# Attention and two MoE layers on one core: decoding of the weights in fewer and denser steps, a third split buffer, output copies after both halves of a PSUM tile

## The chip, the core and the metric

The kernel runs on one core of a Trainium2 chip. Five engines work beside each other, each in the order of its own instructions: TensorE (PE in the profile; PEld is its weight load), VectorE (DVE), ScalarE (ACT), GpSimd (POOL) and SyncE (SP), which here issues every DMA. The metric is the device time of one execution in microseconds.

## The reference

```python
# attention: q, k, v are 4 x 8 x 576 x 64
scores = scale * np.matmul(q, k.transpose(0, 1, 3, 2)) + bias   # bias: a small network of relative positions
attn = np.exp(scores - np.max(scores, axis=-1, keepdims=True))
attn = attn / (np.sum(attn, axis=-1, keepdims=True) + 1e-09)
x = np.matmul(attn, v)                      # as 2304 tokens x 512
h = np.maximum(np.maximum(x @ w1, x @ w2), x @ w3)    # moe1: 512 -> 768
x = h @ w_out                               # 768 -> 512
h = x @ w_in                                # moe2: 512 -> 2048
g = np.where(h > 0.0, h, np.exp(np.minimum(h, 0.0)) - 1.0)
out = g @ w_out2                            # 2048 -> 512
```

The weights of both MoE layers come as float64 and reach the chip as pairs of 32-bit words.

## The kernel before

**Stages.** First the position bias is made, then attention runs in 80 steps (16 pairs of heads, five chunks of rows), then moe1, then moe2. Python code writes the instructions out in order; no scheduler changes it, so the order of the calls is the order on each engine.

**Precision.** Every matrix product is made of three: each operand is split into a high part and a low part, and high x high, high x low and low x high are added in PSUM.

**Decoding.** A block of weights (128 x 512 doubles) is fetched into one of two buffers `raw` (`fetch`, L346). Five VectorE instructions and one of ScalarE turn it into floats (L392 to L402): x_t from the high words, on ScalarE the exponent step L394, t_w or cw_t in four steps, of which the last needs ScalarE's x_t. `split` then writes the high part with ScalarE (L74) and the low part with GpSimd (L80), and `store` sends both to a scratch tensor `scw_...` (L437). `load_w` brings them back into one of six buffers `w_t` (L464) some four products ahead of their use. Splits go to a ring of two buffers `sp2` (sp in the profile). Two kinds don't: a block of w1 that is the very next one needed is split straight into a `w_t` buffer, and w_out of moe1 stays in the tile wo_t. For w_in of moe2 the two halves of a block (keys `("wi", f, 1)` and `("wi", f, 0)`, tile cw_t) get four sums first (L412), and then four splits follow one another: moe2 multiplies by a scheme with sums of sub-matrices.

`decoder` is a generator: each `yield` ends a step, and `pump(k)` advances it by k steps. There are 24 blocks of moe1 (18 of w1, six of w_out) and eight groups of four for moe2. Before, a block costs six steps and a group 32, 400 in all. Attention calls `pump()` in 59 of its steps, on the first twelve blocks alone; `moe1_ev` pumps two steps ahead of each of its evictions, `moe1_out` five behind each. If a load needs a block that isn't decoded, `need` advances the decoder on the spot.

**moe1.** Three passes over 768 tokens. A pass has 18 products (`moe1_mm`, L491: six row blocks, three matrices; 24 instructions each), each into one pair of four pairs of PSUM banks; `moe1_ev` copies the first to a_t on ScalarE (L501), takes the maximum with the other two on VectorE (L503), and splits it into hh and hl. The output stage `moe1_out` (L586, four products of 36 instructions) of one pass runs three products into the next pass, and the last one at the end of moe1; its evictions are xh on ScalarE (L592) and xl on VectorE (L593).

**moe2.** 24 units (three passes, eight blocks of hidden rows). The products L662 go to the two banks Y and X, and VectorE copies them out as c_t, p_t, q_t, u_t. In the first two units each bank is used alternately, and `sums` holds 16 closures that make the four sums of x (e_t on GpSimd, d_t and tt on VectorE and ScalarE): one is called after each of the four turns of the first unit, three after each of the second. The output products L706 add up over the eight units in six banks `acc`: acc[0] and acc[1] are the halves of one two-bank tile (pb), acc[2] and acc[3] of another, acc[4] and acc[5] are tiles of their own. In the last unit of a pass `store_out` copies each to o_t, even ones with VectorE and odd ones with ScalarE, and stores it. The tiles of moe2 take over the memory in which the decoder's buffers lay.

## Time and profile before

| | |
|---|---|
| median of 3 runs | 1043.83 us (1040.75 to 1044.81) |
| the profiled execution | 1043.28 us |
| its span, first to last instruction | 1041.5 us |
| mean granted TensorE clock | 0.989 of 2.4 GHz |
| TensorE busy | 97% of the span |
| DMA, mean over the span | 190 GB/s |

The span leaves out 1.8 us of the execution around the instructions. The clock is that which TensorE was granted, as a share of its full speed; it has two levels, 1.2 and 2.4 GHz. Attention lasts to about 340 us, moe1 to 643 us, moe2 to the end.

### The profile page before, as it was taken

The page shows a single profiled execution, that of the slowest core. Times are in us where ns is not written, and L with a number is a line of the kernel's source. Part 1 is how long each engine was busy: PE and PEld are TensorE (multiplying, and loading weights), DVE is VectorE, ACT ScalarE, POOL GpSimd, SP SyncE. Part 2 cuts the span into 40 slices and gives each one's busy share as a digit, 9 for nine tenths or more (in the row PEclk, how much of TensorE's full clock was granted, in tenths as well). Part 3 has the DMA queues.
Part 4 walks back from the last instruction along what each step waited for, and adds up shares of the span by engine and source line. Part 5 has one row for each costly group of instructions (what it writes and reads, how often), then busy time and mean ns, then how long its engine had stood idle before and what let it go on. Part 6 is the DMA issues. An engine that isn't in the chain of part 4 may idle for free. (4 is left out here: it accounts for less than half of the span.)

```text
span 1041.5 us, 17213 instructions
## 1 busy us (share of the span) xinstructions
PE 1008.3 (97%) x6068; PEld 839.6 (81%) x6068; DVE 691.0 (66%) x1402; ACT 547.1 (53%) x1175; POOL 346.7 (33%) x319
## 2 busy tenths in 40 slices
PE   7999999999999999989998988999999999999997
PEld 3456666666668999989998988879998989889896
DVE  7967778777776699577677755854774356843342
ACT  8978888888885333333232433444444345443443
POOL 0013333333332344335332532522452233522221
PEclk9989999999999999999999999899999999999999
DMA  7741625436232567589767884346557555566552
GB/s 274 270 143 62 224 87 184 143 116 211 96 98 92 171 222 250 166 280 306 275 210 240 293 301 155 111 145 199 175 190 259 183 183 188 192 238 191 170 195 102
DMA packets 67733, 197.65 MB, mean 190 GB/s; under 512 B 9280, under 2 KB 16320, under 8 KB 67648
## 3 DMA queue, kind: packets, MB, share of 16 engines
q1 hardware_dynamic: 67648, 196.56, 56.2%
q8 instruction: 49, 0.80, 0.3%
q14 instruction: 36, 0.29, 0.1%
HBM read 148.16 MB, written 48.37 MB: 189 GB/s over the span
## 5 line engine op out<-in xcount | busy, mean ns | idle before, releaser
L80 POOL TENSOR_TENSOR gl<-t_t,gh 128x384 fp32r<-128x384 f32 x96 | 106.2, 1116 | 246.1 <-ACT gh L74 239.8
L233 DVE CUSTOM_DVE_ANT_0 e_t<-pb,b_t 128x576 f32<-128x576 f32 x144 | 104.1, 756 | 57.1 <-PE pb L224 35.8
L250 POOL TENSOR_SCALAR e_t<-e_t,st_t 128x576 f32<-128x576 f32 x64 | 65.9, 1030 | 225.8 <-DVE st_t L244 213.3
L74 ACT ACTIVATE p<-bk 128x512 f32<-128x512 f32 (+2 forms) x224 | 98.9, 472 | 54.8 <-PE bk L257 54.5
L706 PE MATMUL pb<-w_t,gh 128*128 128x512 f32 x384 | 120.0, 394 | 4.3 <-DVE o_t L76 4.3
L491 PE MATMUL pb<-xh,w_t 128*128 128x384 f32 x448 | 118.4, 340 | 2.7 <-DMA w_t<-scw_w 2.7
L238 ACT ACTIVATE e_t<-e_t,st_t 128x576 f32<-128x576 f32 x144 | 111.7, 776 | 2.2 <-DVE st_t L233 2.2
L491 PE MATMUL bk<-xh,w_t 128*128 128x384 f32 x416 | 109.0, 337 | 3.6 <-DMA w_t<-scw_w 3.0
L684 ACT ACTIVATE t_t<-c_t 128x384 f32<-128x384 f32 x96 | 50.0, 521 | 111.3 <-DVE c_t L675 88.8
L662 PE MATMUL bk<-tt,w_t 128*128 128x384 f32 x528 | 107.5, 338 | 1.0 <-DVE p_t L76 1.0
L662 PE MATMUL bk<-xh,w_t 128*128 128x384 f32 x328 | 96.6, 341 | 6.9 <-DVE c_t L76 6.9
L662 PEld LDWEIGHTS bk<-tt,w_t 128*128 128x128 f32 x528 | 95.0, 188 | 8.8 <-DVE p_t L76 1.4
L491 PEld LDWEIGHTS pb<-xh,w_t 128*128 128x128 f32 x448 | 82.2, 190 | 3.4 <-ACT a_t L501 3.0
L224 PE MATMUL pb<-kq_t 64*128 64x288 f32 x512 | 82.9, 437 | 1.3 <-DVE st_t L233 1.3
L706 PEld LDWEIGHTS pb<-w_t,gh 128*128 128x128 f32 x384 | 70.2, 188 | 13.0 <-DVE o_t L76 6.6
L491 PEld LDWEIGHTS bk<-xh,w_t 128*128 128x128 f32 x416 | 75.4, 188 | 4.0 <-issue 3.3
L491 PE MATMUL pb<-xl,w_t 128*128 128x384 f32 x224 | 76.0, 339 | 0.0
L299 PE MATMUL bk<-p,tv_t 128*64 128x320 f32 (+1 forms) x512 | 76.0, 418 | 0.0
L706 PE MATMUL pb<-w_t,gl 128*128 128x512 f32 x192 | 75.5, 393 | 0.0
L74 ACT ACTIVATE gh<-t_t 128x384 fp32r<-128x384 f32 x96 | 48.9, 519 | 47.2 <-DVE t_t L692 47.2
L692 DVE SCALAR_TENSOR_TENSOR t_t<-t_t,c_t 128x384 f32<-128x384 f32 x96 | 72.1, 769 | 0.8 <-ACT t_t L685 0.5
L662 PEld LDWEIGHTS bk<-xh,w_t 128*128 128x128 f32 x328 | 61.5, 191 | 10.6 <-DVE c_t L76 7.7
(116 smaller groups left out, 2109.4 us busy)
## 6 DMA issues: line engine op xcount, KB each, us to landing
w_t<-scw_w SPq DMA_DIRECT2D x90, 512.0 KB, 4.2
w_t<-scw_wi SPq DMA_DIRECT2D x74, 512.0 KB, 4.2
scw_wi<-sp SPq DMA_DIRECT2D x26, 512.0 KB, 2.9
scw_w<-sp SPq DMA_DIRECT2D x22, 512.0 KB, 5.2
raw<-wo SPq DMA_DIRECT2D x22, 512.0 KB, 4.3
scr<-o_t SPq DMA_DIRECT2D x36, 288.0 KB, 3.9
kq_t<-tkq SPq DMA_DIRECT2D x16, 640.0 KB, 4.8
raw<-wm SPq DMA_DIRECT2D x18, 512.0 KB, 3.7
```

The costliest lines, as they stand in the source:

```text
L74: nc.scalar.activation(dst, src, AF.Copy)
L80: e.tensor_tensor(out=dst, in0=src, in1=hi.bitcast(F32), op=ALU.subtract)
L224: mm(PB[h][:, o], t[r, 640 + 128 * c:768 + 128 * c], t[r, k0:k0 + 288], start=True, stop=True)
L233: nc.vector.tensor_tensor_reduce(out=E[s][:, 576 * h:576 * h + 576], in0=PB[h][:, 224:800], in1=BT[n // 4, c, h], op0=ALU.add, op1=ALU.min ...
L238: nc.scalar.activation(e, e, AF.Exp, bias=st[:, h:h + 1], scale=-1.0, accum_out=st[:, 2 + h:3 + h])
L250: nc.gpsimd.tensor_scalar(e, e, r, 1.0, op0=ALU.mult, op1=ALU.mult)
L299: mm(XO[64 * h:64 * h + 64, 0:w], v[:, 128 * k + 64 * h:128 * k + 64 * h + 64], ps[h][:, k, :], start=(k == 0), stop=False, skip_group_che ...
L491: mm(ps[blk][:, 0:NB], wt[:, ks], xt[:, kk, t0:t0 + NB], start=(j == 0), stop=(j == 11))
L662: mm(ps, w[wt][:, ks], b[xt][:, kk], start=(start and j == 0), stop=(stop and j == 5), skip_group_check=True)
L684: nc.scalar.activation(t, c, AF.Relu, scale=-1.0)
L692: pend.append([lambda: nc.vector.scalar_tensor_tensor(out=t, in0=t, scalar=-1.0, in1=c, op0=ALU.add, op1=ALU.max), last])
L706: mm(acc[t], g[:, ts], w[k], start=(f == 0 and i == 0 and j == 0), stop=(f == NU - 1 and i == 1 and j == 2))
```

## The change

A block's last empty step goes away, so that it costs five steps and a group 31 (368 in all), and each of the last three splits of a burst gets one more step ahead of it. The evictions of moe1's products pump three and two steps, those of its output stages four. `fetch` is called a step later, ahead of the last of the five VectorE instructions instead of behind the fourth. After the attention, every third split that isn't written in place goes to a third buffer, sp3. `store_out` gets a tile of its own for each 128 x 512 block (four instead of two of twice the size) and is called for both halves of a two-bank tile behind the product into the second. In moe2's first two units two closures of `sums` are called a turn.

```diff
@@ -349,6 +349,7 @@
 
     lim = [12]
     WPRE2 = []
+    NSP = [0]
     SCW, WO, HERE, WS, WN = {}, [], set(), [], [0, 0]
 
     def split(key, src, c0=0):
@@ -361,7 +362,9 @@
             WN[0] += 1
             HERE.add(key)
         else:
-            sp2 = wpre.tile([128, 2, 512], F32R, tag="sp2", name="sp2", bufs=2)
+            pool, tag = (WPRE2[0], "sp3") if WPRE2 and NSP[0] % 3 == 2 else (wpre, "sp2")
+            sp2 = pool.tile([128, 2, 512], F32R, tag=tag, name=tag, bufs=2 if tag == "sp2" else 1)
+            NSP[0] += bool(WPRE2)
         hi, lo, src = sp2[:, 0, c0:], sp2[:, 1, c0:], src[:, c0:]
         parts = [partial(hi_of, "a", hi, src), partial(lo_of, "p", lo, src, hi)]
         if key[0] != "wo":
@@ -397,8 +400,8 @@
             nc.vector.scalar_tensor_tensor(out=t, in0=hi, scalar=-0x80000000, in1=t, op0=ALU.bitwise_and, op1=ALU.bitwise_or)
             yield
             nc.vector.scalar_tensor_tensor(out=t, in0=lo, scalar=29, in1=t, op0=ALU.logical_shift_right, op1=ALU.bitwise_or)
+            yield
             fetch()
-            yield
             nc.vector.tensor_tensor(out=t, in0=t, in1=x, op=ALU.bitwise_or)
             if key[0] != "wi":
                 split(key, dst)
@@ -412,10 +415,11 @@
                     nc.vector.tensor_tensor(out=d, in0=a, in1=b, op=op)
                 for p in range(4):
                     yield
+                    if p:
+                        yield
                     split(("wi", key[1], p), cw[:, p], 256 if p == 3 and key[1] > 1 else 0)
                     if len(todo) > 1:
                         store()
-            yield
             yield
             if len(todo) > 1:
                 store()
@@ -495,7 +499,7 @@
         ps = PS.pop((th, m, w))
         for blk in range(2):
             p = ps[blk][:, 0:NB]
-            pump(2)
+            pump(3 - blk)
             if w == 0:
                 A1[blk] = wpre.tile([128, NB], F32, tag="a", name="a_t", bufs=3)
                 nc.scalar.activation(A1[blk], p, AF.Copy)
@@ -591,7 +595,7 @@
                     xh, xl = XH[:, m, t0:t0 + NB], XL[:, m, t0:t0 + NB]
                     nc.scalar.activation(xh, p, AF.Copy)
                     nc.vector.tensor_tensor(out=xl, in0=p, in1=xh.bitcast(F32), op=ALU.subtract)
-                    pump(5)
+                    pump(4)
 
         with tc.manual_schedule():
             order = [(th, m, w) for th in range(3) for m in range(NM1) for w in range(3)]
@@ -705,24 +709,24 @@
         for j, (g, k) in enumerate(((GH, 0), (GH, 1), (GL, 0))):
             mm(acc[t], g[:, ts], w[k], start=(f == 0 and i == 0 and j == 0), stop=(f == NU - 1 and i == 1 and j == 2))
 
-    def store_out(blk, t, o):
+    def store_out(blk, t):
+        o = mp.tile([128, 512], F32, tag="o", name="o_t", bufs=4)
         r0 = blk * TB + 128 * t
         w = 256 if t == 5 else 512
         for c0 in range(0, 512, w):
             cs = slice(c0, c0 + w)
-            hi_of("a" if t % 2 else "v", o[:, t % 2, cs], acc[t][:, cs])
-            nc.sync.dma_start(out[r0:r0 + 128, cs], o[:, t % 2, cs])
+            hi_of("a" if t % 2 else "v", o[:, cs], acc[t][:, cs])
+            nc.sync.dma_start(out[r0:r0 + 128, cs], o[:, cs])
 
     acc = PAIR[0] + PAIR[1] + PAIR[2]
-    OT = {}
 
     def outs(u, i, ts, w):
         for t in ts:
             moe2_out(u, i, t, w, acc)
             if u[1] == NU - 1 and i == 1:
-                if t % 2 == 0:
-                    OT[0] = mp.tile([128, 2, 512], F32, tag="o", name="o_t", bufs=2)
-                store_out(u[0], t, OT[0])
+
+                for d in ((t - 1, t) if t in (1, 3) else (t,) if t > 3 else ()):
+                    store_out(u[0], d)
 
     sums = [fn for i in range(4) for fn in comb(0, i + 1)]
     with tc.manual_schedule():
@@ -748,7 +752,7 @@
                         elu(u, i, q, c)
                         if pre:
                             outs(pre, i, range(3 * q, 3 * q + 3), v)
-                        for _ in range(3 if pre else 1):
+                        for _ in range(2):
                             sums.pop(0)()
                     loads(2 if pre else 1)
                 continue
```

**A burst of splits.** ScalarE in moe1's second pass, at the four splits of the third group (f = 2); sp_... are the split buffers, cw_t the block, a_t and hh evictions. Before:

```order
L74 ACTIVATE sp_5028<-cw_t 128x512
L74 ACTIVATE sp_5033<-cw_t 128x512
L501 ACTIVATE a_t<-bk_866 128x384
L74 ACTIVATE sp_5066<-cw_t 128x512
L74 ACTIVATE sp_5071<-cw_t 128x256
L394 ACTIVATE x_t<-x_t,rebias 128x512
L74 ACTIVATE hh<-a_t 128x384
L74 ACTIVATE sp_5117<-t_w 128x512
```

After:

```order
L74 ACTIVATE sp_4885<-cw_t 128x512
L74 ACTIVATE sp_4917<-cw_t 128x512
L74 ACTIVATE hh<-a_t 128x384
L74 ACTIVATE sp_4925<-cw_t 128x512
L74 ACTIVATE hh<-a_t 128x384
L74 ACTIVATE sp_4961<-cw_t 128x256
L397 ACTIVATE x_t<-x_t,rebias 128x512
L505 ACTIVATE a_t<-pb_100 128x384 x2
L74 ACTIVATE sp_5006<-t_w 128x512
```

The splits of the burst were in two pairs with one eviction between; now evictions stand between the second, third and fourth, and this burst comes two row blocks earlier in the pass.

**The end of moe1.** ScalarE in the last output stage, up to its last eviction; xh are the evictions of that stage. Before:

```order
L74 ACTIVATE sp_6429<-cw_t 128x512
L592 ACTIVATE xh<-bk_866 128x384
L74 ACTIVATE sp_6436<-cw_t 128x512
L74 ACTIVATE sp_6441<-cw_t 128x512
L74 ACTIVATE sp_6446<-cw_t 128x256
L592 ACTIVATE xh<-pb_100 128x384
L394 ACTIVATE x_t<-x_t,rebias 128x512
L74 ACTIVATE sp_6497<-t_w 128x512
L592 ACTIVATE xh<-pb_100 128x384
L394 ACTIVATE x_t<-x_t,rebias 128x512
L74 ACTIVATE sp_6512<-t_w 128x512
L592 ACTIVATE xh<-pb_99 128x384 x2
```

After, from the last product ahead of the stage:

```order
L505 ACTIVATE a_t<-bk_865 128x384
L505 ACTIVATE a_t<-bk_866 128x384
L74 ACTIVATE hh<-a_t 128x384 x2
L596 ACTIVATE xh<-bk_863 128x384
L596 ACTIVATE xh<-bk_864 128x384
L596 ACTIVATE xh<-bk_865 128x384
L596 ACTIVATE xh<-bk_866 128x384
L596 ACTIVATE xh<-pb_100 128x384 x2
L596 ACTIVATE xh<-pb_99 128x384 x2
```

Six splits and two exponent steps stood between these evictions; now there is none.

**The output.** TensorE in the last pass, the first four of the six output products of the last half unit (pb_100 holds acc[0] and acc[1], pb_99 the next two), with what an instruction waits for. Before:

```order
L706 MATMUL pb_100<-w_t,gh 128x512 [waits DMAHW4_49,Activation_49]
L706 MATMUL pb_100<-w_t,gh 128x512
L706 MATMUL pb_100<-w_t,gl 128x512 [waits Pool_49]
L706 MATMUL pb_100<-w_t,gh 128x512 [waits DVE_49]
L706 MATMUL pb_100<-w_t,gh 128x512
L706 MATMUL pb_100<-w_t,gl 128x512
L706 MATMUL pb_99<-w_t,gh 128x512 x2
L706 MATMUL pb_99<-w_t,gl 128x512
L706 MATMUL pb_99<-w_t,gh 128x512 [waits DVE_49]
L706 MATMUL pb_99<-w_t,gh 128x512
L706 MATMUL pb_99<-w_t,gl 128x512
```

After:

```order
L710 MATMUL pb_100<-w_t,gh 128x512 [waits DMAHW2_49,Activation_49]
L710 MATMUL pb_100<-w_t,gh 128x512
L710 MATMUL pb_100<-w_t,gl 128x512 [waits Pool_49]
L710 MATMUL pb_100<-w_t,gh 128x512 x2
L710 MATMUL pb_100<-w_t,gl 128x512
L710 MATMUL pb_99<-w_t,gh 128x512 x2
L710 MATMUL pb_99<-w_t,gl 128x512
L710 MATMUL pb_99<-w_t,gh 128x512 x2
L710 MATMUL pb_99<-w_t,gl 128x512
```

The second product into each two-bank tile waited for VectorE; now it does not.

With the denser steps twelve blocks instead of almost ten are decoded in the attention; the last six blocks of w1, which were split straight into weight buffers, are now ready before their turn and go through the scratch tensor; and the last step of decoding falls three products ahead of the last output stage.

## Rows read from the trace of the kernel before

**Rows 1.** The page: busy us (share) x instructions of each engine.

```profile
PE 1008.3 (97%) x6068; PEld 839.6 (81%) x6068; DVE 691.0 (66%) x1402; ACT 547.1 (53%) x1175; POOL 346.7 (33%) x319
```

**Rows 2.** TensorE's waits, whole span: total us, times, longest us.

```profile
PE bk L662 <- DVE c_t L76: 6.9, 2, 5.6
PE pb L706 <- DVE o_t L76: 4.3, 6, 1.0
PE bk L491 <- DMA w_t<-scw_w: 3.0, 1, 3.0
PE pb L491 <- DMA w_t<-scw_w: 2.7, 1, 2.7
PE bk L586 <- ACT hh L74: 1.9, 1, 1.9
PE bk L586 <- POOL hl L80: 1.5, 1, 1.5
```

**Rows 3.** Windows: us, then each engine's busy us (x instructions), TensorE's clock, DMA share, GB/s.

```profile
460.00:470.00 10.00, 7.80 (x36) 7.83 (x37) 9.79 (x14) 4.36 (x9) 4.90 (x5) 0.83 1.01 370
620.00:630.00 10.00, 10.00 (x50) 10.00 (x50) 7.53 (x14) 3.44 (x6) 0.77 (x2) 0.84 0.59 186
650.00:660.00 10.00, 6.88 (x28) 6.89 (x29) 6.51 (x9) 4.52 (x9) 2.86 (x2) 0.66 0.30 105
```

**Rows 4.** The same view over most of moe1.

```profile
345.00:612.00 267.00, 261.31 (x1497) 260.73 (x1496) 196.85 (x300) 91.81 (x174) 107.27 (x87) 0.99 0.72 243
```

**Rows 5.** ScalarE's waits from 345 to 612 us: total us, times, longest us.

```profile
ACT sp L74 <- DMA scw_wi<-sp: 35.5, 18, 3.8
ACT sp L74 <- DMA scw_w<-sp: 29.1, 6, 6.5
```

**Rows 6.** Timeline of SyncE's DMA queue at 457 us: start, us, instruction.

```profile
457.19 0.46 SPq L464 DMA_DIRECT2D w_t<-scw_w  x1
```

**Rows 7.** Timeline of TensorE and VectorE at moe2's start: start, us, instruction [idle before, releaser].

```profile
643.23 0.33 PE L662 MATMUL bk<-xh,w_t 128*128 128x384 f32 x1
652.50 0.56 DVE L76 COPY c_t<-bk 128x384 f32<-128x384 f32 x1 [2.30 <-DMA scw_w<-sp]
653.12 0.69 PE L662 MATMUL bk<-xh,w_t 128*128 128x384 f32 x1 [5.57 <-DVE c_t L76]
679.82 0.45 PE L662 MATMUL bk<-xh,w_t 128*128 128x384 f32 x1 [1.36 <-DVE c_t L76]
```

**Rows 8.** Timeline of TensorE: a product of moe1, an output stage, the next product.

```profile
413.59 0.34 PE L491 MATMUL pb<-xh,w_t 128*128 128x384 f32 x1
417.75 0.34 PE L586 MATMUL pb<-hh,wo_t 128*128 128x384 f32 x1
442.73 0.33 PE L491 MATMUL pb<-xh,w_t 128*128 128x384 f32 x1
```

**Rows 9.** Lines from 364 to 394 us, the last from 200 to 300 us: xcount | busy us, mean ns.

```profile
L397 DVE SCALAR_TENSOR_TENSOR t_w<-raw,t_w 128x512 int32<-128x512 int32 x7 | 8.5, 1212 | 0.2
L399 DVE SCALAR_TENSOR_TENSOR t_w<-raw,t_w 128x512 int32<-128x512 int32 x6 | 6.4, 1072 | 0.1
L402 DVE TENSOR_TENSOR t_w<-t_w,x_t 128x512 int32<-128x512 int32 x6 | 5.6, 930 | 0.6
L395 DVE TENSOR_SCALAR t_w<-raw 128x512 int32<-128x512 int32 x7 | 4.3, 612 | 0.0
L392 DVE TENSOR_SCALAR x_t<-raw 128x512 int32<-128x512 int32 x7 | 2.9, 420 | 0.5 <-DMA raw<-wm 0.5
L503 DVE TENSOR_TENSOR a_t<-bk,a_t 128x384 f32<-128x384 f32 x5 | 2.7, 548 | 0.0
L80 POOL TENSOR_TENSOR w_t<-t_w,w_t 128x512 fp32r<-128x512 f32 x6 | 9.5, 1576 | 13.3 <-ACT w_t L74 13.3
L397 DVE SCALAR_TENSOR_TENSOR t_w<-raw,t_w 128x512 int32<-128x512 int32 x4 | 2.8, 696 | 0.0
```

**Rows 10.** Lines of ScalarE from 345 to 612 us.

```profile
L394 ACT ACTIVATE x_t<-x_t,rebias 128x512 int32<-128x512 int32 x39 | 27.9, 716 | 15.5 <-DVE x_t L392 15.5
```

## The prediction

> **What bounds the kernel now.** I began with the busy times of the engines: TensorE is busy for 1008.3 of 1041.5 us [rows 1], so a change that leaves its products alone can only win back its idle time and the time at a low clock. The list of what TensorE waited for comes next [rows 2]; all its places that this change can reach lie behind the attention, and the longest are c_t (6.9 us, at the start of moe2), o_t (4.3), two late weights (3.0 and 2.7), and hh and hl at moe1's last product (1.9 and 1.5). The third view is the granted clock around these gaps [rows 3]: after the late weight at 460 it is 0.83 for ten microseconds, after hh and hl 0.84, after c_t 0.66. Each gap is paid a second time there.
>
> Why the weights are late is seen on the other engines. Over most of moe1 VectorE is busy for 197 of 267 us [rows 4], though it carries the decoding, and ScalarE waits 35.5 + 29.1 us for the stores of split buffers to land before it may write the next high part [rows 5]. With two buffers, the third of four splits in a row waits for the first one's store. Whatever follows on ScalarE waits too: PSUM copies, and the exponent step without which VectorE cannot end its block. SyncE is in order as well, so a load stands behind such a store: the first load after moe1's first output stage was issued only at 457.19 [rows 6], and its product is the one that waited 2.7 us [rows 2].
>
> **The change, part by part.** Times are first those of the profiled execution (1043.28 us, 0.55 under the median), then shifted.
>
> *Output copies.* Of the six stalls on o_t, two in each pass over the tokens, each comes from a product into the second half of a PSUM tile behind the copy of its first half. The order now puts both copies behind both products, and no product of the last list waits for VectorE. 4.3 us go [rows 2]. In the last pass the copies run closer together, and ScalarE's now waits for VectorE's; I give 0.4 back. Gain 3.9, bounds 2.5 and 4.3.
>
> *End of moe1.* Before, 40 steps of decoding are in the last output stage and the product ahead of it still has some; after, the last step falls three products before that stage. The program needs 368 steps instead of 400 (24 blocks of six, now five, and eight groups of 32, now 31); the attention offers 59, the 54 products four each, now five, and the 24 evictions of the output stages five each, now four. The evictions that make hh and hl then stand first on VectorE, ScalarE and GpSimd. The price is 1.9 + 1.5 [rows 2] plus (1 - 0.84) x 10 = 1.6 of clock [rows 3]: 5.0. Bounds 3.4 and 5.0.
>
> *Start of moe2.* TensorE began moe2 at 643.23 but waited 5.57 us until 653.12 for the first c_t, copied at 652.50; VectorE itself waited there for the last store of a split buffer, whose memory c_t takes over [rows 7]. With the stores tens of microseconds earlier that goes. In rows 3, 3.4 us of clock are lost from 650 to 660, but up to half of the 3.1 us before the restart fell in the idle time, so 1.85 counts. Together with the next stall on c_t, 1.36 at 679.82 [rows 7], 6.9 + 1.85 = 8.75. Not all comes back: VectorE works almost without a break from 652.50 to the copy that ends this second stall, 27.3 us. Starting after one of moe2's products (half as many instructions as one of moe1's, 2.08 us), at 645.3, it ends at 672.6; TensorE, without its stalls, wants that copy at 679.82 - 8.75 = 671.07. 1.5 remain. Two sums a turn instead of one and three move this work, they don't lessen it. Gain 7.2, bounds 3.0 (the stall comes back as several) and 8.75.
>
> *Decoding in moe1.* What can return is 3.0 + 2.7 [rows 2] and at most 1.7 of clock [rows 3]: 7.4. Against it stands the new pace. A block of weights takes five steps instead of six, a product offers five instead of four. A product lasts 4.16 us and an output stage 24.98 [rows 8]. From the third product to the fourteenth every product carries a whole block. VectorE's five instructions took 1.21 + 1.07 + 0.93 + 0.61 + 0.42 = 4.25 us at that pace, and two evictions in two products of three add 0.73 [rows 9]: 4.98 against 4.16, a lag of 0.82 a product, 9.8 over twelve, some 2 more because the second eviction now stands behind all five. PSUM has four pairs, so TensorE waits only when a lag passes three products, 12.5 us: just not. Then come blocks whose four splits give VectorE less work, and the lag falls.
>
> Over the whole stretch, 49 products and two output stages last 253.8 us. In the window of rows 4 there are 39 blocks [rows 10], which took VectorE 197 us with their sums and evictions; 44 blocks make about 220. With the 12.5 of slack, VectorE may idle 46 us before TensorE loses any; before, it idled 70. The third buffer and the step between splits must therefore take a third of that away. They should take more: a burst's third split now needs the store three splits back, not two, and comes two steps later.
>
> The extra traffic is counted from the order: 42 fetches, 52 stores and 49 loads where 39, 45 and 43 stood, because six blocks of w1 that were split straight into weight buffers now go through memory. At 128 x 1024 words, 0.524 MB each (six stores half as much), that is 73.4 MB, in 253.8 us 289 GB/s, against 243 [rows 4]; for seven products of the first pass it is 1.57 MB a product, 378 GB/s, where rows 3 reach 370. This costs latency. The fetch moved a step later lets a load pass it now and then; it holds the same wait for VectorE, and nothing but the next block stands behind it. I leave 3 us of waits in moe1. Gain 4.4, bounds -17 (rival one) and 7.4.
>
> The Trainium skill (DMA: Bandwidth & Descriptors, Where 436 GB/s comes from) gives about 358 GB/s to a core against memory; at that figure the seven products take an estimated 1.6 us longer. Rows 3 show 370.
>
> *Attention.* It now decodes two more blocks: ten VectorE instructions, four of ScalarE, two of GpSimd, in slots that were empty. TensorE hides them as it hides the others; bounded by nothing and the about 4.25 us of one block. I take 0.5.
>
> Sum: 3.9 + 5.0 + 7.2 + 4.4 - 0.5 = 20.0, so 1023.3 for the profiled execution and 1024 for the median.
>
> **The rivals.** Each keeps the other terms; without any moe1 wait the time would be 1021.
>
> *One: the waits on split buffers persist.* If the denser steps use up what the third buffer gives and VectorE idles its 70 us again, 220 + 70 - 266 = 24 us of waits come back in moe1, and the time is 1045, no change. It starts to cost at 46 us of idling. For it speak the stores' longer landing at 289 GB/s; against it, that a burst is spread over seven steps instead of four.
>
> *Two: GpSimd holds VectorE up for longer.* Place: the twelve products of one block each. The instruction at L397 took 1.21 us there and 0.70 in the attention, that at L399, of the same form, 1.07: 0.89 a block are already in the 4.25, while a low part keeps GpSimd for 1.58 [rows 9]. If a block loses the whole of it, 0.69 more, the lag is 12 x 1.51 + 2 = 20.1, so 7.6 us of waits and 1.7 of clock: 1030. For it speaks that after the change GpSimd has its low parts while VectorE is full; against it, that the loss seen is about half.
> The Trainium skill (SBUF — State Buffer, Who interferes with whom) has the rule: a VectorE instruction with two SBUF inputs and a GpSimd one that reads SBUF exclude each other for the whole instruction. It speaks against this change; the rows show the exclusion, and by the rule's full price it is this rival.
>
> *Three: the start of moe2 stays bound by VectorE.* Four sums stand in the first unit, where TensorE has four half products, 8.3 us. If copies of c_t queue behind them, 5 us of waits and 1.85 of clock come instead of 1.5: 1029. Against it, the work ahead of the last copy is the same.
>
> *Four, slower: transfers run full.* The place is all of moe1. If no more than R is carried for long, 73 MB last 73/R, and from R = 249 GB/s down the kernel is more than 0.5% slower: 73.4 / 0.249 = 295 us, 28.7 beyond the 266 allowed. At 243, the mean of before, it is 1056. Against it stands a window with 370 [rows 3]; for it, that this window was only ten microseconds long.
>
> **How the numbers follow.** The forecast (1017 to 1030) has 0.61, rival one 0.14 (0.06 of it above 0.5% faster, 0.08 within), rival two 0.10, three 0.08, four 0.07. Half a per cent, 5.2 us, is about what a measurement of this kernel can tell from no change. Faster by more: 0.61 + 0.06 + 0.10 + 0.08 = 0.85; within: 0.08; slower: 0.07. The range 1017 to 1038 has at its low end every wait gone, at its high end rival one at two thirds; it leaves out 0.04 below and the rest of rival one and all of rival four, 0.15, above.
>
> **What would show it.** Right: no o_t in TensorE's waits; no DMA into split buffers in the last output stage of moe1; hh and hl gone; first c_t copy about 2 us after moe2's first product; ScalarE's waits on split stores at a third of 65 us. Wrong: TensorE waiting for a_t copies (VectorE) between the sixth and the sixteenth product, or for weights through all of moe1; sp waits as long as before. The prediction fails most easily at the pace in moe1, since its 46 us allowance is worked out from a total and not from each stage.

## The result and the profile after

The changed kernel takes 1027.21 us (median of four runs, 1025.42 to 1029.79) beside 1043.21 for the kernel before (four runs, 1040.75 to 1044.81). The ratio is 0.9851, its 95% interval 0.9818 to 0.9883. That is inside the range, 3.2 us above the forecast of 1024. The profiled execution takes 1025.84 us with a span of 1023.9, so 17.6 us less span than before, where the prediction's sum was 20.0.

Busy times on the page of the changed kernel, the row that answers to [rows 1]:

```profile
PE 1003.1 (98%) x6068; PEld 836.8 (82%) x6068; DVE 701.9 (69%) x1402; ACT 547.5 (53%) x1175; POOL 353.1 (34%) x319
```

TensorE's waits over the whole span (total us, times, longest us). They answer to [rows 2]: o_t, hh and hl are gone, c_t is halved and comes in four pieces, and late weights still cost 4.0.

```profile
PE pb L495 <- DMA w_t<-scw_w: 3.8, 2, 2.2
PE bk L666 <- DVE c_t L76: 3.6, 4, 2.0
PE bk L495 <- DMA w_t<-scw_w: 0.2, 1, 0.2
```

The late weights are all in the first pass, which lost nothing before. TensorE's timeline there (start, us, instruction, idle before it):

```profile
393.75 0.42 PE L495 MATMUL bk<-xh,w_t 128*128 128x384 f32 x1 [0.16 <-DMA w_t<-scw_w]
399.69 0.42 PE L495 MATMUL pb<-xh,w_t 128*128 128x384 f32 x1 [1.53 <-DMA w_t<-scw_w]
406.33 0.41 PE L495 MATMUL pb<-xh,w_t 128*128 128x384 f32 x1 [2.24 <-DMA w_t<-scw_w]
```

ScalarE's waits for the split buffers from 335 to 612 us answer to [rows 5]: 28.8 us for stores instead of 64.6. What it waits for most at these splits is now VectorE's decoding.

```profile
ACT sp L74 <- DVE t_w L405: 34.3, 16, 3.4
...
ACT sp L74 <- DMA scw_w<-sp: 21.2, 8, 4.1
...
ACT sp L74 <- DMA scw_wi<-sp: 7.6, 8, 3.5
```

Windows of the changed kernel (columns as in [rows 3]; the first answers to [rows 4]): VectorE is busy for 224 of 267 us, transfers run at 278 GB/s, the last output stage moves no data, and the clock falls only once around moe2's start, to 0.88 in the window shown and 0.95 in the next ten microseconds.

```profile
345.00:612.00 267.00, 263.07 (x1515) 262.20 (x1514) 224.06 (x327) 100.00 (x188) 120.28 (x94) 1.00 0.81 278
620.00:630.00 10.00, 10.00 (x60) 10.00 (x59) 1.36 (x3) 1.35 (x3) 0.00 (x0) 1.00 0.00 0
390.00:400.00 10.00, 8.31 (x47) 7.73 (x46) 8.50 (x12) 3.88 (x7) 3.75 (x3) 1.00 0.84 251
...
660.00:670.00 10.00, 7.97 (x34) 6.81 (x33) 8.25 (x9) 4.21 (x9) 5.70 (x4) 0.88 0.28 81
```

**Stage by stage.** Three products of moe1 stand among the attention's last work; the fourth, the first behind it, begins anywhere from 340.6 to 343.7 us in kernels that carry the same attention, so from here on lengths of stages are compared. They are differences of TensorE's starts in each profiled execution: from that product ("start") to moe1's first output stage ("first pass"; 18 products, 75.0 without a wait), from it to moe2's first product ("moe1"; 287.2 without a wait), from there to the product that waited at 679.82 in [rows 7] ("start of moe2"), and from there to the end of the span ("rest").

| kernel | median us | start | first pass | moe1 | start of moe2 | rest |
|---|---|---|---|---|---|---|
| before | 1043.21 | 342.75 | 75.00 | 300.48 | 36.59 | 361.68 |
| changed | 1027.21 | 343.38 | 79.67 | 291.89 | 31.87 | 356.76 |
| e1 in place | 1018.07 | 343.70 | 74.99 | 287.22 | 31.87 | 356.11 |
| e5 ring of two | 1039.66 | 343.46 | 83.23 | 308.61 | 31.87 | 356.76 |
| e6 old output | 1031.20 | 342.91 | 82.12 | 294.35 | 31.87 | 361.87 |
| e8 old pace | 1019.32 | 340.59 | 74.99 | 288.80 | 31.87 | 356.04 |
| e9 before + third buffer | 1029.19 | 342.72 | 74.99 | 287.52 | 35.34 | 361.72 |
| e14 more traffic | 1019.81 | 343.61 | 74.99 | 287.21 | 31.88 | 356.40 |
| e7 sums one and three | 1021.75 | 342.24 | 81.02 | 293.24 | 28.80 | 356.42 |
| e2 copies by ScalarE | 1019.67 | 340.68 | 82.82 | 295.05 | 27.27 | 356.00 |
| e10 in place, copies | 1013.18 | 343.09 | 74.99 | 287.45 | 27.28 | 355.98 |
| e12 in place, early sums | 1020.54 | 340.74 | 74.99 | 287.22 | 34.32 | 355.22 |
| e13 old pace, copies, early sums | 1013.58 | 342.19 | 74.99 | 287.88 | 27.27 | 355.06 |
| e15 in place, sums one and three | 1017.74 | 340.84 | 74.99 | 289.35 | 28.81 | 356.50 |

Between the first two rows, attention lost 0.63, moe1 gained 8.59, the start of moe2 4.72 and the rest 4.92: 17.6. Within moe1 the first pass lost 4.67, the other two won 4.5 and 3.3 back, and the last output stage fell from 30.49 to 24.98. The 4.67 is of one execution: with the same code up to the end of moe1, the first pass takes 81.02 us in e7, 82.12 in e6 and 82.82 in e2, where the granted clock from 400 to 410 us, behind the late weights, is 0.83, 0.88 and 0.83; in the changed kernel's profile it stays at 1.00.

### The profile page after: what moved, and what is told of

It is laid out like the page before. It is cut to its first block, busy times and chain, and to the rows that moved or that the text cites. A ratio compares the mean times of both kernels' runs of the same rounds, so it can differ in the third digit from the quotient of the medians.

```text
span 1023.9 us, 17230 instructions
## 1 busy us (share of the span) xinstructions
PE 1003.1 (98%) x6068; PEld 836.8 (82%) x6068; DVE 701.9 (69%) x1402; ACT 547.5 (53%) x1175; POOL 353.1 (34%) x319
## 4 chain that ended last, share of the span: by engine, by line
PE 92%; DVE 3%; DMA 3%; ACT 1%; issue 0%; SPq 0%; ACTq 0%; DVEq 0%
PE bk L666 16%; PE pb L710 12%; PE pb L495 10%; PE bk L495 9%; PE pb L224 8%; PE bk L299 7%; PE bk L710 6%; PE bk L257 4%; PE bk L590 4%; PE pb L590 4%; PE bk L269 3%; PE pb L186 2%; PE pbb L186 2%; PE pb L226 2%; PE bk L302 2%; DMA scw_w<-sp 2%
## 5 line engine op out<-in xcount | busy, mean ns | idle before, releaser
L80 POOL TENSOR_TENSOR gl<-t_t,gh 128x384 fp32r<-128x384 f32 x96 | 109.0, 1146 | 245.2 <-ACT gh L74 240.0
L495 PEld LDWEIGHTS bk<-xh,w_t 128*128 128x128 f32 x416 | 75.4, 188 | 1.2 <-ACT xf L320 0.7
L224 PEld LDWEIGHTS pb<-kq_t 64*128 64x128 f32 x512 | 46.2, 190 | 29.0 <-issue 9.7
```

The source lines that it names most:

```text
L80: e.tensor_tensor(out=dst, in0=src, in1=hi.bitcast(F32), op=ALU.subtract)
L224: mm(PB[h][:, o], t[r, 640 + 128 * c:768 + 128 * c], t[r, k0:k0 + 288], start=True, stop=True)
L495: mm(ps[blk][:, 0:NB], wt[:, ks], xt[:, kk, t0:t0 + NB], start=(j == 0), stop=(j == 11))
```

## The experiments

Intervals are for the ratio to the kernel before.

### What holds the first pass up: e1, e14

e1 changes only the order of decoding. Two more w_out blocks come ahead of the last six blocks of w1, so that each of these is again the next one needed and is split straight into its weight buffer. It is still stored for the later passes; only its load falls away.

```diff
-    DQ += w1s[:12] + wos[:3] + w1s[12:] + wos[3:]
+    DQ += w1s[:12] + wos[:5] + w1s[12:] + wos[5:]
```

> The changed kernel with one edit: two more blocks of w_out are decoded ahead of the last six blocks of w1, so that these fall due when they can be split straight into their weight buffers again (six loads and their waits for stores fewer). Theory A: the 3.9 us of late weights in moe1's first pass come from these six blocks going through memory, each load standing in SyncE's queue until its store has landed (26.4 us of such waits). Then TensorE's waits for w_t are gone, the first pass is 4 to 5 us shorter, and the span is 1019 to 1020 (1023.9 now). Rival B: the pace of one block a product makes everything behind VectorE late; then the waits stay at 3 to 4 us or come back as waits for a_t, and the span stays within 1.5 us of 1023.9.

Measured: 1018.07 us, ratio 0.9765 [0.975, 0.9779]. The waits for weights are gone, the first pass takes 74.99 us, and moe1 loses nothing: the six loads are the cause of the 4.67 us. (The medians are 9.1 apart, the two profiled spans 5.0; the changed kernel's profile is of one of its shorter executions, 1025.84 us, and e1's of its longest, 1020.73.) How they are late is seen in SyncE's DMA queue in the changed kernel (start, us, instruction; w_t is a load, scw_w a store):

```profile
372.47 0.32 SPq L468 DMA_DIRECT2D w_t<-scw_w  x1
372.89 0.38 SPq L441 DMA_DIRECT2D scw_w<-sp  x1
...
378.22 0.32 SPq L468 DMA_DIRECT2D w_t<-scw_w  x1
378.59 0.43 SPq L441 DMA_DIRECT2D scw_w<-sp  x1
...
383.93 0.32 SPq L468 DMA_DIRECT2D w_t<-scw_w  x1
384.30 0.42 SPq L441 DMA_DIRECT2D scw_w<-sp  x1
...
389.61 0.32 SPq L468 DMA_DIRECT2D w_t<-scw_w  x1
```

Each load waits for the store just ahead of it to land, and the next store is issued only behind that load. One such round takes 5.7 us, while a product takes 4.16 [rows 8], so each block comes 1.5 us later against its product than the one before. SyncE's waits from 340 to 430 us (total, times, longest) add these six up:

```profile
SPq L468 <- DMA scw_w<-sp: 26.4, 6, 5.8
```

The rival to this reading was bandwidth: the six loads also bring 3.1 MB. e14 puts as many bytes back into e1, as six stores that nobody waits for.

```diff
+    SCR = [dram.tile([128, 2, 512], F32, name=f"scr_{i}") for i in range(6)]
...
         if key in HERE:
             HERE.remove(key)
+            if key[1] in (4, 5):
+                nc.sync.dma_start(SCR[3 * key[1] + key[2] - 12], XH[:, 0:2, 0:512].bitcast(F32))
```

> The kernel of e1 (six blocks of w1 split in place, first pass over the tokens without a wait, 75.0 us to its first output stage) with six more stores of 0.524 MB, one with each of these six blocks: a piece of xh, which nobody writes and nobody waits for, to memory. They carry as many bytes as the six loads that the changed kernel has and e1 hasn't, at nearly the same places of SyncE's queue, but no load stands behind a store. Theory (the first pass lost 4.7 us since each of the six loads stood in SyncE's queue until its own block's store had landed): first pass 75.0 to 75.5 us, median 1017.5 to 1019.5, that is within 1.5 us of e1's 1018.07. Rival (it lost them since the transfers were full): weights are late by 2 us or more in the first pass, which takes 77.5 us or more, and the median is 1021 to 1026.

Measured: 1019.81 us, ratio 0.9777 [0.9757, 0.9798]. The median is 1.74 above e1's, a little more than I had allowed, but the intervals overlap, moe1 lasts 287.21 as in e1, and no product waited for a weight. In the windows from 370 to 400 us, where the rounds lie, e14 moves 285, 318 and 317 GB/s, the changed kernel 220, 304 and 251:

```profile
380.00:390.00 10.00, 10.00 (x60) 10.00 (x59) 9.69 (x15) 4.04 (x8) 4.85 (x4) 1.00 0.92 318
390.00:400.00 10.00, 10.00 (x59) 10.00 (x59) 9.69 (x13) 3.84 (x7) 5.82 (x4) 1.00 0.90 317
...
410.00:420.00 10.00, 10.00 (x59) 10.00 (x58) 8.43 (x12) 4.64 (x9) 6.76 (x6) 1.00 1.02 394
```

So the bytes are not the cause; e14 adds them as stores, and the same bytes as loads that nobody waits for were not run. Whether a block's longer way alone would do, or the order in SyncE's queue is needed, was not separated by a run; the round of 5.7 us is read from the rows.

### What the third buffer and the pace are worth: e5, e9, e8

e5 is the changed kernel without the third buffer.

```diff
-            pool, tag = (WPRE2[0], "sp3") if WPRE2 and NSP[0] % 3 == 2 else (wpre, "sp2")
+            pool, tag = (WPRE2[0], "sp3") if WPRE2 and NSP[0] % 3 == 7 else (wpre, "sp2")
```

> The changed kernel with the ring of two split buffers of before, all else as changed. Theory: the third buffer is what cut ScalarE's waits for stores from 64.6 to 28.8 us; without it they are above 50 us, VectorE waits for ScalarE again, and late weights or copies cost 3 to 8 us in passes two and three of moe1 (span 1027 to 1032). Rival: the steps between the splits do it alone; then ScalarE's waits stay under 40 us and the span within 1.5 us of 1023.9.

Measured: 1039.66 us, ratio 0.9961 [0.9946, 0.9976]. moe1 takes 16.7 us more than with the buffer, 13.0 of them in passes two and three, where I had given 3 to 8, and 8.1 more than before the change. ScalarE's waits (335 to 612 us) and TensorE's (whole span) in e5:

```profile
ACT sp L74 <- DMA scw_w<-sp: 45.5, 10, 6.6
ACT sp L74 <- DMA scw_wi<-sp: 37.1, 21, 4.1
```

```profile
PE bk L495 <- DMA w_t<-scw_w: 6.8, 3, 4.4
...
PE pb L495 <- DVE cw_t L405: 4.3, 1, 4.3
```

82.6 us of waits for stores, more than the 64.6 of [rows 5]: the denser steps with more time between the splits don't replace the buffer. Against the kernel before, the first pass takes 8.2 us more (the six loads stand in it here too), passes two and three 5.3 more, and the last output stage, without a step of decoding, 5.5 less: it lasts 24.98. This is the prediction's rival one, brought about by hand; it gave 1045 for it.

e9 is the reverse, the kernel before with the third buffer and nothing else of the change.

```diff
+    NSP = [0]
...
-            sp2 = wpre.tile([128, 2, 512], F32R, tag="sp2", name="sp2", bufs=2)
+            pool, tag = (WPRE2[0], "sp3") if WPRE2 and NSP[0] % 3 == 2 else (wpre, "sp2")
+            sp2 = pool.tile([128, 2, 512], F32R, tag=tag, name=tag, bufs=2 if tag == "sp2" else 1)
+            NSP[0] += bool(WPRE2)
```

> The kernel before with one part of the change alone: the third split buffer, which the eight groups of splits take in turn with the two others. Pace, the place of the fetch, the spacing of the splits, the output copies and the sums stay as before. Theory: the third buffer alone brings most of what moe1 gained (ring of two against the change: 12 us). ScalarE's waits for stores fall from 64.6 us to 25 or less, the waits for late weights (5.7 us) and on hh and hl (3.4) go with the clock lost behind them; o_t stays at 4.3 and the first copy of moe2 is early: span 1024 to 1030, median about 1028. Rival: a third buffer without the longer spacing of the splits and without fewer steps doesn't suffice; ScalarE waits 45 us or more, and the span is 1034 to 1040.

Measured: 1029.19 us, ratio 0.9865 [0.9847, 0.9883], span 1027.3. One edit takes 13.0 us out of moe1, which then lasts 287.52, close to the 287.2 and 4.4 less than in the changed kernel. ScalarE waits 12.1 + 5.9 us for stores, less than in the changed kernel. What is left is at the start of moe2 and in the output, as TensorE's waits in e9 say (p_t is a copy shortly behind the start of moe2):

```profile
PE bk L665 <- DVE c_t L76: 5.3, 2, 4.0
PE pb L709 <- DVE o_t L76: 4.3, 6, 1.0
...
PE bk L665 <- DVE p_t L76: 1.0, 1, 1.0
```

With 400 steps, decoding still goes on at the end of moe1. The start of moe2 takes 35.34 us here and 28.80 in e7 (below), which has the same order of the sums and 368 steps at the new pace. That difference of 6.5 us is what decoding that ends before moe2 brings. The fewer steps do it without the new pace: e8 starts moe2 in the 31.87 us of the changed kernel.

e8 is the changed kernel (368 steps, third buffer) at the pace of before.

```diff
-            pump(3 - blk)
+            pump(2)
...
-                    pump(4)
+                    pump(5)
```

> The changed kernel with the pump counts of before (two ahead of each eviction of a product, five behind each of an output stage), all else as changed: 368 steps, 395 offered, so some 13 steps of decoding lie in the last output stage again. Theory: the waits on hh and hl come back with their clock (5.5 us in the stage's 30.5 against 25.0), the first c_t stays early, and the first pass loses its late weights, because the last blocks of w1 fall due later; span 1023 to 1026. Rival: the denser pace is what gives the gain in passes two and three too; then waits for weights behind the output stages (2.7 and 3.0 before) come back as well, span 1028 to 1032.

Measured: 1019.32 us, ratio 0.9774 [0.9757, 0.979]. That is 7.9 us under the changed kernel (6.6 in the profiled spans, of which 2.8 lie ahead of moe1). The first pass takes 74.99 us, and TensorE's only wait for a weight is 1.3 us, in the second pass. But it isn't the pace as such that costs the changed kernel this time: at four steps a product five of the six blocks of w1 come late enough again to be split straight into their weight buffers, as ScalarE's lines from 345 to 612 us show (none in the changed kernel, six in e1):

```profile
L74 ACT ACTIVATE w_t<-t_w 128x512 fp32r<-128x512 f32 x5 | 3.2, 635 | 11.8 <-DVE t_w L405 9.0 <-issue 2.8
```

e1 keeps the five steps and has 1018.07, with overlapping intervals, and its moe1 is 1.6 us shorter than here. So the denser pace costs only by way of the six loads, and without them it brings 1.6 us in moe1 at most. I had expected hh and hl to come back, since decoding reaches into the last output stage again. It does, as a window of e8 shows, but the stage still lasts 24.98 us:

```profile
610.00:620.00 10.00, 10.00 (x59) 10.00 (x58) 6.01 (x11) 4.16 (x8) 5.26 (x5) 1.00 0.50 196
```

### The start of moe2: e7, e12, e2, e10

e7 is the changed kernel with the sums as before, one a turn in the first unit and three in the second.

```diff
-                        for _ in range(2):
+                        for _ in range(3 if pre else 1):
```

> The changed kernel with the sums at the start of moe2 as before: one after each activation of the first unit and three after each of the second, in place of two and two. Theory (VectorE's amount of work ahead of the last copy is the same, so the waits on c_t are only spread differently): the waits on c_t are 3 to 4.2 us in all, the first of them shorter, median 1026 to 1028.5, no change that can be measured. Rival (the two sums in the first unit were what held its copies up): waits on c_t 2 us or less, and median 1023 to 1025.5.

Measured: 1021.75 us, ratio 0.9791 [0.9768, 0.9815]. The theory that only the places of the waits would move was wrong: c_t falls from 3.6 to 1.4 us, and the start of moe2 from 31.87 to 28.80. Why is on VectorE's timeline. First the changed kernel, from the first copy of c_t on (VectorE, then GpSimd in the same stretch):

```profile
637.60 0.56 DVE L76 COPY c_t<-bk 128x384 f32<-128x384 f32 x1
638.08 0.95 DVE L653 TENSOR_TENSOR d_t<-xh 128x768 f32<-128x768 f32 x1
639.13 0.96 DVE L655 TENSOR_TENSOR d_t<-d_t,e_t 128x768 f32<-128x768 f32 x1
640.01 0.55 DVE L76 COPY c_t<-bk 128x384 f32<-128x384 f32 x1
640.48 0.55 DVE L696 SCALAR_TENSOR_TENSOR t_t<-t_t,c_t 128x384 f32<-128x384 f32 x1
642.44 0.96 DVE L80 TENSOR_TENSOR tt<-d_t,tt 128x768 fp32r<-128x768 f32 x1 [1.42 <-ACT tt L74]
643.32 0.55 DVE L76 COPY c_t<-bk 128x384 f32<-128x384 f32 x1
643.79 0.90 DVE L696 SCALAR_TENSOR_TENSOR t_t<-t_t,c_t 128x384 f32<-128x384 f32 x1
644.61 2.62 DVE L653 TENSOR_TENSOR d_t<-xh,tt 128x768 f32<-128x768 f32 x1
647.33 1.58 DVE L655 TENSOR_TENSOR d_t<-d_t,e_t 128x768 f32<-128x768 f32 x1
648.84 0.55 DVE L76 COPY c_t<-bk 128x384 f32<-128x384 f32 x1
...
665.05 1.56 DVE L655 TENSOR_TENSOR d_t<-d_t,e_t 128x768 f32<-128x768 f32 x1
666.54 0.55 DVE L76 COPY c_t<-bk 128x384 f32<-128x384 f32 x1
```

```profile
642.90 1.36 POOL L80 TENSOR_TENSOR gl<-t_t,gh 128x384 fp32r<-128x384 f32 x1 [5.44 <-ACT gh L74]
644.23 2.18 POOL L652 TENSOR_TENSOR e_t<-xl,tt 128x768 f32<-128x768 f32 x1
```

A sum is four closures: a difference, an addition, the high part on ScalarE, the low part on VectorE. With two a turn, the high and the low part fall into the same turn, and VectorE stands 1.42 us for ScalarE with the next copy of c_t behind it; this happens in every second turn (4.3 us in three of them). In the other turns the difference and the addition both stand ahead of the next copy: 5.5 us pass from 643.32 to 648.84. In e7's first unit the high and the low part fall into different turns (the last two lines are from its second unit):

```profile
641.92 0.56 DVE L76 COPY c_t<-bk 128x384 f32<-128x384 f32 x1 [0.19 <-PE bk L666]
...
644.00 0.56 DVE L76 COPY c_t<-bk 128x384 f32<-128x384 f32 x1 [0.56 <-PE bk L666]
...
644.93 1.78 DVE L80 TENSOR_TENSOR tt<-d_t,tt 128x768 fp32r<-128x768 f32 x1
646.63 0.54 DVE L76 COPY c_t<-bk 128x384 f32<-128x384 f32 x1
...
663.68 0.55 DVE L76 COPY c_t<-bk 128x384 f32<-128x384 f32 x1
...
664.61 0.95 DVE L655 TENSOR_TENSOR d_t<-d_t,e_t 128x768 f32<-128x768 f32 x1
```

Here the copies wait for TensorE, and the low part waits for nothing. The amount of work differs too, which my theory denied: the fourth addition (L655) stands ahead of the eighth and last copy of c_t in the changed kernel (665.05, 666.54) and behind it in e7 (664.61, 663.68). From the first copy to the eighth VectorE takes 28.94 us in the changed kernel and 25.87 in e7, the whole 3.07 us by which the stage differs. Its waits are 1.2 us of that (4.3 for ScalarE against 3.1 for TensorE and GpSimd); the other 1.9 are work, with the addition of 1.56 in it. Which of the two would be enough by itself was not separated by a run. e7's median is 5.5 us below the changed kernel's, more than the 3.1 of this stage; the two profiles, of one execution each, don't show where the rest is.

e12 (in place as e1) puts two closures ahead of the first activation, where VectorE seemed free.

```diff
+                if not pre:
+                    sums.pop(0)()
+                    sums.pop(0)()
...
-                        for _ in range(2):
+                        for _ in range(min(2, len(sums))):
```

> The changed kernel with the order of loading of e1, and two of the sums that VectorE makes at the start of moe2 put ahead of the first product's activation, where VectorE otherwise has nothing to do. Compared with e1 (1018.07, four waits on c_t of 3.6 us). Theory (VectorE's amount of work before the last copy bounds the start): about 1.2 us of work comes out of the way of the later copies; waits on c_t 2 to 2.8 us, median 1016.5 to 1017.5. Rival (the sums delay the first copy by what they take): the first wait grows by what the others lose, and the median is 1017.8 to 1019.

Measured: 1020.54 us, ratio 0.9784 [0.9762, 0.9805]; the rival's effect came, at a price above both ranges. The waits on c_t rise to 4.5 us (longest 2.6): in e1 the first three make 1.6 and the last 2.1, here 4.2 and 0.3. The clock is 0.83 from 640 to 650, and the start of moe2 takes 34.32 us.

e2 gives the copies of c_t in the first two units to ScalarE; e10 has the same edit on top of e1.

```diff
-                        hi_of("v", c, ps)
+                        hi_of("a", c, ps)
```

> The changed kernel with one edit: ScalarE instead of VectorE makes the high copies c_t of the first two units of moe2. With the other order of loading the same edit took 4.9 us (e1 1018.07, e10 1013.18), 3.6 of them waits on c_t. Theory (the start of moe2 doesn't depend on what moe1 lost, and the two add up): no wait on c_t, the waits for late weights in the first pass stay at about 4 us, median 1021 to 1023.5. Rival (part of e10's gain was in moe1): waits on c_t go, but the median is 1024 or more.

> The changed kernel with the order of loading of e1 (no w1 block through memory in place of wo blocks), and ScalarE instead of VectorE makes the high copies c_t of the first two units of moe2. Compared with e1 (1018.07, four waits on c_t of 3.6 us). Theory (VectorE has more work than TensorE gives it time for at the start of moe2): eight copies of about 0.55 us leave VectorE, the waits on c_t fall to 1 us or less, median 1014.5 to 1016. Rival (the chain of each unit, not VectorE's amount of work, sets it: ScalarE's own steps of the activation stand ahead of the copies in its queue): waits on c_t stay at 2.5 us or more and the median is 1017 to 1020.

Measured: e2 1019.67 us, ratio 0.9776 [0.9753, 0.98]; e10 1013.18, ratio 0.972 [0.9698, 0.9741]. No wait on c_t is left in either, and the start of moe2 is 27.3 us in both. Both are 1.3 below what I gave. e10 is 4.9 below e1 and 14.0 (1.4%) below the changed kernel: the fastest run here. In its windows at the start of moe2, VectorE is busy for 9 of 10 us and TensorE is full:

```profile
640.00:650.00 10.00, 10.00 (x53) 9.14 (x52) 9.00 (x7) 5.47 (x12) 7.44 (x5) 1.00 0.44 145
650.00:660.00 10.00, 10.00 (x52) 8.94 (x50) 9.01 (x8) 5.68 (x11) 5.25 (x5) 1.00 0.30 94
```

In e2 the six loads are there, and its first pass takes 82.82 us, with 5.5 us of waits: 3.3 for loads and 2.2 for a block that VectorE was still decoding. In the changed kernel, e7, e2 and e6 the first output stage begins at 423.05, 423.26, 423.50 and 425.03, for starts from 343.38 down to 340.68: what an execution is ahead at the start it loses again, to late weights and to the lower clock behind them.

### The output copies: e6

e6 is the changed kernel with the output copies of before (`store_out`, not shown, writes to halves of one tile again).

```diff
-                for d in ((t - 1, t) if t in (1, 3) else (t,) if t > 3 else ()):
-                    store_out(u[0], d)
+                if t % 2 == 0:
+                    OT[0] = mp.tile([128, 2, 512], F32, tag="o", name="o_t", bufs=2)
+                store_out(u[0], t, OT[0])
...
```

> The changed kernel with the output copies of before (two tiles of two halves, each copy right behind its product). Theory: the six waits on o_t return, 4.3 us and their restarts: span 1028 to 1029.5. Rival: the end of the kernel is set by copies and stores whatever TensorE does, and the gain of the last pass is given back in waits for output buffers; then the span is under 1027.

Measured: 1031.2 us, ratio 0.9885 [0.987, 0.99], 4.0 us above the changed kernel. TensorE's six waits on o_t are back with 4.3 us, and the rest takes 361.87, 5.1 more than in the changed kernel, a little above what I gave. Behind the start of TensorE's last instruction the changed kernel is the slower one: its last store lands 4.1 us later, e6's 3.3.

### Combinations: e15, e13

e15 is e1 and e7 together, e13 is e8 with the edits of e12 and e2.

> The changed kernel with two edits together: the order of loading of e1, so that no block of w1 goes through memory between its split and its product in the first pass, and the sums of e7, one and three a turn as before. Theory (the two losses of the change are independent, 4.7 us in the first pass and 3.1 at the start of moe2): moe1 from its first product to the first of moe2 lasts 287.2 us (291.9 in the changed kernel), the start of moe2 28.8 us to the X product of its unit 3 (31.9 there), the waits on c_t are 1.4 us, and the median is 1014 to 1016.5. Rival (VectorE comes into the start of moe2 with another backlog when moe1 loses nothing): the start takes 31 us or more and the median is 1017 to 1019.

> The changed kernel with the old pace of decoding (as e8, 1019.32), the copies c_t of the first two units of moe2 by ScalarE and the two sums ahead of the first activation. Theory: the two parts of the start of moe2 add to the old pace; its waits on c_t go from 3.6 to 1 us or less, span 1013 to 1015, median about 1016. Rival: decoding reaches into the last output stage with the old pace, so VectorE and ScalarE start moe2 later, and nothing comes of it: median 1018.5 or more.

Measured: e15 1017.74 us, ratio 0.9758 [0.974, 0.9775]; e13 1013.58, ratio 0.9719 [0.9699, 0.9739]. In e15 the start of moe2 is 28.81 us as in e7, so the two losses are independent. But its moe1 takes 2.1 us more than the 287.2: in this execution it starts 2.9 us earlier than in e1, and two waits came up in the second and third pass, 1.2 us on a_t and 0.5 on a weight. e12 has the same moe1, starts at 340.74 and loses nothing there, so the early start alone is not the reason; it stays open. I gave 1014 to 1016.5; the rival's median came, without the longer start of moe2 that it named. e13 has no wait on c_t, equals e10 within its interval, and is 2.4 below the 1016 that I gave; its rival did not come.

## Why the prediction was right, and where its terms were off

The sum was 20.0 and the profiled pair shows 17.6. By the prediction's own terms:

*Output copies*, 3.9: e6 puts the six waits back and shows 4.0 in the median and 5.1 in the rest of the traces, with 0.8 lost at the end, where the sum gave 0.4 back. The 4.92 us that the rest gained against the kernel before also hold a wait on p_t of 1.0 us, which the sum left out, less the low clock behind the start of moe2.

*End of moe1*, 5.0: 5.51 measured. The size was right, and the reason was one of two. The prediction put hh and hl down to steps of decoding in the last stage. e5 bears it out: with two buffers and no step there, the stage lasts 24.98. But in e8 such steps are there and it lasts 24.98 as well; in e9, with all 400 steps and the old pace, 25.25. So the third buffer does this without the other, and either is enough.

*Start of moe2*, 7.2: 4.72 measured, the one term that was clearly mis-sized. The first half held: the first copy comes 2.3 us after moe2's first product (637.60 and 635.27), and e7 with the old order of the sums gains 36.59 - 28.80 = 7.8. The step that failed is the sentence "Two sums a turn instead of one and three move this work, they don't lessen it": 1.5 us were to remain, and 3.07 more than in e7 did. The new order puts a low part directly behind the high part that it needs, a new wait between two engines, and one addition more ahead of the last copy. Rival three rested on the same mistake: "the work ahead of the last copy is the same" is wrong by that addition, and with two closures a turn two sums, not four, stand in the first unit. Its place and effect came all the same (5 us of waits and 1.85 of clock named; 3.6 of waits came, and 1.7 of clock by the windows from 660 to 680, which lies behind the stage and counts in the rest). e10 shows that VectorE was the bound there.

The price of VectorE's work beside GpSimd belongs here. In the rows above, L653 takes 2.62 us beside GpSimd's L652 and 0.95 us at 638.08, in the 5.44 us that GpSimd is idle ahead of 642.90. The Trainium skill (SBUF — State Buffer, Who interferes with whom) has it that a VectorE instruction with two SBUF inputs and a GpSimd one that reads SBUF exclude each other. By that, L653 would start behind L652, at 646.41, and end at 647.36; it ended at 647.23, so here the full price was paid. For moe1 the prediction took about half from [rows 9]. That half is a mean over two cases: of the instructions at L397, the one that starts at 375.06, ahead of GpSimd's at 375.15, takes 0.69 us, and the one at 379.43, behind GpSimd's low part from 379.00 to 380.54, takes 1.67. No product of moe1 waited for an a_t in the changed kernel: rival two did not come.

*Decoding in moe1*, 4.4 with 3 us of waits left: 3.1 measured, 4.0 us of late weights left. The net was nearly right, in part by luck: the 3 us left for the latency of more traffic happened to cover most of a loss of another kind. The second and third pass gained 7.7 us, as much as all waits there with their clock, and the first pass, for which no loss was named, lost 4.67. The prediction had seen the six blocks of w1 that go through memory and counted their bytes; e14 shows that as many bytes in stores hold no product up, and e1 that the loss goes with the six loads. The sign named for ScalarE's waits, a third of 65 us, was missed with 28.8: 21.2 us of waits on the stores to scw_w remain. The allowance did hold: VectorE idles 43 of 267 us, with 46 allowed, at 224 us of work for the 220 reckoned. Transfers ran at 278 GB/s for 289, so rival four had nothing to stand on. The Trainium skill (DMA: Bandwidth & Descriptors, Where 436 GB/s comes from) puts the limit of a core's traffic with memory at about 358 GB/s, half of what it gives for two; the windows of this kernel, which runs on one core, go above that, with 394 in ten microseconds of e14.

What carried the gain was the buffer, not the pace. The prediction said that the third buffer "and the step between splits" must take a third of the idling away; e9 shows that the buffer does it alone, e5 that the step without the buffer does not. e8 is 7.9 us faster at the old pace and e1 9.1 at the new one, both without most or all of the six loads: the pace lost by them, and its gain is the 1.6 us in moe1 between e8 and e1 at most. Fewer steps pay where decoding ends, at the start of moe2 (6.5 us between e9 and e7).

*Attention*, 0.5: 0.63 in this pair. moe1's start varies by 3 us between executions, but it does so with the clock from 60 to 70 us (last section). Where that was 0.66 to 0.68, moe1 starts at 342.91 to 343.70 in six kernels with the new attention and at 342.75 and 342.72 in the two with the old one, 0.2 to 1.0 us apart, which bears the size out.

## What to carry to other kernels

When a schedule gets denser, look for the work that is now ready too early: a rule such as "the very next block goes straight to its buffer" then takes its other branch, and the detour through memory can cost more than the wait that was removed. A load that stands in the same queue behind the store that it needs makes one round of both, and that round must be shorter than the work that it feeds. And when work is regrouped into turns, check for each turn whether an engine now waits inside it for another, and count what stands ahead of the last result that somebody needs; equal work in total says nothing of either.

## What was not expected of the hardware

A load of 0.5 MB behind the store of the same bytes made rounds of 5.7 us, although the core's transfers ran at only 220 to 304 GB/s in the windows around them; in e14 they reached 318 in the same stretch. With equal waits on c_t (3.6 us in four pieces, the longest 2.0 or 2.1) the granted clock from 660 to 670 us was 0.88 in the changed kernel and 1.00 in e1 and e8, so the price of the same gaps differs between executions. And moe1 started up to 3.1 us apart behind the same attention (340.59 in e8, 343.70 in e1). This goes with the clock around 60 us; first e8, then e1:

```profile
60.00:70.00 10.00, 9.31 (x60) 6.38 (x60) 7.98 (x27) 8.71 (x23) 3.96 (x4) 1.00 0.54 194
60.00:70.00 10.00, 9.58 (x39) 6.25 (x40) 6.20 (x22) 6.28 (x17) 2.59 (x3) 0.66 0.35 125
```

It is 1.00 in the four executions that start moe1 at 340.59 to 340.84 (e8, e2, e12, e15), 0.83 in the two at 342.2 (e7, e13), and 0.66 to 0.68 in the eight at 342.72 and later. TensorE's two waits just ahead, 0.95 and 0.39 us, are the same in e8 and e1; why the clock then fell in one and not in the other stays open.
